# One round of eight small matmuls for the first Fourier stage of the second tokens' pairs, over other PSUM banks

## The chip, the cores and the metric

The kernel runs on one core of one Trainium2 chip. The metric is the device time of one execution in microseconds (us); lower is better. A change of 0.5% of this kernel's time is about 3.65 us.

## The reference

One token sequence (2048 tokens of 448 features) is normalised, and three things are added up: the input, a state-space convolution of the normalised input, and a gated linear unit of it. The convolution is written with a Fourier transform of double length. Cut to what matters:

```python
def _A_ref(u, log_A_real, A_imag, C_real, C_imag, log_dt, D_skip):   # S4D convolution
    dt = jnp.exp(log_dt)
    A = -jnp.exp(log_A_real) + 1j * A_imag
    C = (C_real + 1j * C_imag) * dt[:, None]
    P = jnp.exp((A * dt[:, None])[:, :, None] * pos[None, None, :])
    K = 2.0 * jnp.einsum("dn,dnl->dl", C, P).real                    # (448, 2048) from 256 modes
    Kf, Uf = jnp.fft.rfft(K, 2 * L), jnp.fft.rfft(u_t, 2 * L)
    y = jnp.fft.irfft(Uf * Kf, 2 * L)[:, :, :L]
    return y.transpose(0, 2, 1) + u * D_skip

def _B_ref(x, w_gate, w_up, w_down):                                 # gated unit, 448 -> 1792 -> 448
    return (sigmoid(x @ w_gate) * (x @ w_up)) @ w_down

x = A_u                                     # (1, 2048, 448)
xn = _layernorm(x)
return x + _A_ref(xn, ...) + _B_ref(xn, ...)
```

## The kernel before

Two generators, `conv()` for the convolution and `glu()` for the gated unit, are drawn from in turn, by fixed shares of progress, so that their instructions are recorded interleaved. The compiler's scheduler then puts each engine's instructions in one order and hands out the PSUM and SBUF buffers; on the chip each engine runs its own list in that order, and semaphores hold it where data or a buffer is missing. A matmul in float32 shows as two records in the trace.

**The gated unit.** The tokens go in two halves of 1024, each as two groups of 512 (`t` = 0, 1). `gate` (line 705) makes for one block of 128 hidden columns the two products `gu` of 512 tokens (11 matmuls each), `th` (tanh, ScalarE), `hf` (VectorE), and the split of `hf` into `hh` (ScalarE) and `hl` (VectorE). The down projection (`po`, line 817) sums over a group of blocks per 128 tokens, and VectorE adds it to `acc` (line 822). At the end of the first half lies one group, `cross`, of two blocks, in which the second 1024 tokens are also prepared, two blocks of 128 tokens ("a pair", b = 8, 10, 12, 14) at a time: `pair_norm` (normalise), `pair_turn` (transposes at line 209, split at lines 215 to 222) and `pair_first`, the subject here. `pair_first` 8 and 10 are called between the two products of a gate, 12 and 14 between two blocks of the down projection.

**The kernel of the convolution.** `kgen` makes the convolution's kernel in 56 steps, and is under way during `cross`. A step has: phases into the two-bank PSUM tile `tr` (two matmuls, line 532), from which ScalarE makes the tile `S` of sines (lines 540, 541, 542, which read `tr`, then 543); VectorE's three products `Et`, `Et`, `Ft` (lines 597 to 599); 64 records of small matmuls into `ko` (line 613). Powers `pm` (line 446) and magnitudes `me`, `mf` (GpSimd, line 510; two squarings by ScalarE, line 523) come ahead of them. There are two tiles `S` (`S0`, `S1`), so the sines of a step wait until VectorE is done with those of two steps before. Every fourth step `ko` is copied to `ks`, and `first_stage` (line 558) turns it with 32 small matmuls into the banks `kp` and `kq`.

**PSUM.** The eight banks are: four of the tag `gu`, which the gates, the down projection, `kq`, `pair_turn` and `pair_first` share; two of `tr`; one `ko`; one `kp`.

**The first Fourier stage.** `x_first_stage(to, xn, g)` multiplies 32 of the 128 partitions (group `g`) of the two token blocks of a pair with `wx`, in two matmuls of 32 rows by 64 columns by 448. For the first 1024 tokens `x_spec` does it in two goes of two groups each, through `tr`. For the second, `pair_first` takes four `gu` banks, one a group, copies each with ScalarE (line 688), two of them into one tile `x1` that shares its buffer with the gate weights (`wraw`), two into tiles that share theirs with the down weights (`rd`), and ScalarE's queue issues for each copy two stores to `x1_d` (line 690), eight a pair. The spectra stage, last in the kernel, reads `x1_d`.

Of the kernel before, what the change touches and what calls it, by code (L numbers as in the profile page):

```python
# [11 lines left out]
F32 = mybir.dt.float32  # L12
# [8 lines left out]
D = 448  # L21
# [19 lines left out]
RB = 2  # L41
# [87 lines left out]
def s4d_glu_kernel(ctx, tc, io):  # L129
    nc = tc.nc  # L130
# [20 lines left out]
    wx = const.tile([128, 64], F32, name="wx")  # L151
# [26 lines left out]
    psg = ctx.enter_context(tc.tile_pool(name="psg", bufs=1, space=PSUM))  # L178
    pg = ctx.enter_context(tc.tile_pool(name="pg", bufs=1, side="left"))
# [91 lines left out]
    def row(b, g):  # L271
        return 32 * (b // 4 % 2) + 8 * g + 4 * (b // 8) + b % 4

    def x_first_stage(to, xn, g):

        s = slice(32 * g, 32 * g + 32)
        for i in range(2):
            nc.tensor.matmul(to[64 * i : 64 * i + 64], wx[s], xn[i][s], start=True, stop=True)

    def x_spec(xn, b0):  # L280

        for p in range(2):
            x1 = slots[("x1a", "x1b", "x1c")[x1s[0] % 3]]
            x1s[0] += 1
            ps = psc[-1].tile([128, 2, 512], F32, name="tr", bufs=1)
            with tc.issue_after(glu_mm[0].ins):
                for j in range(2):
                    x_first_stage(ps[:, j, :D], xn, 2 * p + j)
            nc.scalar.copy(x1, ps[:, :, :D])
            for i in range(2):  # L290
                r = row(b0 + i, 2 * p)
                nc.sync.dma_start(x1_d[:, r : r + 9 : 8], x1[64 * i : 64 * i + 64])
            yield WX
# [386 lines left out]
    def pair_first(b, xns):  # L680

        x1 = pg.tile([128, 2, D], F32, name="x1", tag="wraw", bufs=1)
        pss = [psg.tile([128, 512], F32, name="gu", bufs=4) for _ in range(4)]
        for g in range(4):
            x_first_stage(pss[g][:, :D], xns, g)
        for g in range(4):
            to = x1[:, g] if g < 2 else pg.tile([128, D], F32, name="x1", tag="rd", bufs=RB)
            nc.scalar.copy(to, pss[g][:, :D])
            for i in range(2):
                nc.scalar.dma_start(x1_d[:, row(b + i, g)], to[64 * i : 64 * i + 64])  # L690

# [34 lines left out]
    def glu():  # L726
        stores, later = [], []
        for half in range(2):
# [4 lines left out]
            for fs_ in ORDER[half]:  # L733
# [8 lines left out]
                if cross:  # L742
                    xts = {b: pair_load(b) for b in range(8, 16, 2)}
                    step = lambda f_, b: f_(b, xts[b])
                    mid = [(pair_norm, 8), None, (pair_first, 8), (pair_first, 10)]
                    end = [(), ((pair_turn, 8), (pair_norm, 10)), ((pair_turn, 10), (pair_norm, 12)), ((pair_turn, 12), (pair_norm, 14))]
                    downs = {(0, 0): (pair_first, 12), (0, 1): (pair_turn, 14), (0, 3): (pair_first, 14)}
# [360 lines left out]
    xq, psc, raws, acl, marks, slots, pqs = list(x_first), [], [], [], [None, None], {}, []  # L1108
# [6 lines left out]
    while any(g is not None for g in gens):  # L1115
# [3 lines left out]
        i = min(live, key=lambda i: done[i] / total[i])  # L1119
# [33 lines left out]
```

## Time and profile before

| | |
|---|---|
| median of 3 runs | 729.95 us (728.79 to 732.33) |
| profiled execution | 734.12 us |
| its span, first to last instruction | 732.3 us |
| mean granted TensorE clock | 0.973 |
| TensorE busy | 680.6 us, 93% |
| VectorE busy | 567.3 us, 77% |
| ScalarE busy | 420.8 us, 57% |
| GpSimd busy | 377.3 us, 52% |

Shares of the whole span mix stages with different limits: the start loads and normalises, then the gated unit runs beside `kgen` (to about 540 us), then beside the spectra stage. The four calls of `pair_first` run between 296 and 346.4 us. PE in the lines of the profile is TensorE's matmuls, PEld its weight loads, DVE VectorE, ACT ScalarE, POOL GpSimd, SP SyncE; a "q" behind a name is the engine's own instruction queue, which also issues transfers.

### The profile page before, as it was taken

Reading aid. Unit: us, or ns where it says so; the run is one execution under the profiler, and the core shown is the slowest. Engines: PE = TensorE matmul, PEld = TensorE weight load, DVE = VectorE, ACT = ScalarE, POOL = GpSimd, SP = SyncE. Lnnn points to the kernel's source line nnn. Section 1 sums busy time; section 2 is a strip of 40 time slices with the busy share of each in tenths; the row PEclk is TensorE's granted clock in tenths of the full one; section 3 lists DMA queues with packets and bytes.
Section 4 is the critical chain, followed back from the end, with each engine's and each line's share of the span. In section 5 each row is a group of like instructions: output and inputs, shape, how many; then the busy total and the mean of one; then the engine's idle time right before and its main releaser. Section 6 shows DMA issues by size and latency. Waiting matters only on the chain.

```text
span 732.3 us, 19070 instructions
## 1 busy us (share of the span) xinstructions
PE 680.6 (93%) x7780; PEld 535.8 (73%) x7780; DVE 567.3 (77%) x776; ACT 420.8 (57%) x650; POOL 377.3 (52%) x423
## 2 busy tenths in 40 slices
PE   2898799997998999999999999999999999989994
PEld 1665688786876887566878887888877787766783
DVE  5799996799989999998498988986955555654553
ACT  3646364678587778997388678768633312313310
POOL 2120027799887788786557856767843003251001
PEclk9998899999999999997999999999999999999998
DMA  9946328435314544553952322232359999999756
GB/s 202 227 111 199 80 82 276 146 104 186 126 51 154 176 155 136 157 151 120 267 179 98 93 97 96 76 102 96 70 160 294 265 233 239 217 227 250 178 138 162
DMA packets 93287, 116.76 MB, mean 159 GB/s; under 512 B 12177, under 2 KB 81169, under 8 KB 92945
## 3 DMA queue, kind: packets, MB, share of 16 engines
q1 hardware_dynamic: 83888, 95.08, 48.1%
q10 hardware_dynamic: 6736, 14.57, 6.3%
q0 software_dynamic: 2576, 5.90, 3.3%
q8 instruction: 61, 1.00, 0.6%
q14 instruction: 26, 0.20, 0.1%
HBM read 70.75 MB, written 44.76 MB: 158 GB/s over the span
## 4 chain that ended last, share of the span: by engine, by line
PE 60%; DVE 17%; DMA 6%; ACT 6%; issue 5%; SPq 3%; POOL 1%; ACTq 0%; DVEq 0%; POOLq 0%
PE gu L705 23%; PE po L817 15%; PE sp L899 7%; PE ko L613 6%; PE pv L926 4%; PE tr L532 3%; DVE Ft L599 2%; DVE Et L598 2%; DVE Et L597 2%; DVE hl L723 2%; DMA acc_d<-acc 1%; DMA sx<-x_d 1%; DVE wl L760 1%; DVE hf L716 1%; PE kq L558 1%
## 5 line engine op out<-in xcount | busy, mean ns | idle before, releaser
L510 POOL TENSOR_TENSOR me<-me,pm 128x32 f32<-128x32 f32 (+1 forms) x168 | 144.4, 860 | 88.4 <-DVE Et L598 76.3
L510 POOL TENSOR_TENSOR mf<-mf,pm 128x64 f32<-128x64 f32 (+1 forms) x112 | 119.5, 1067 | 4.9
L705 PE MATMUL gu<-xh,wh 128*128 128x512 f32 x336 | 101.1, 407 | 3.0 <-ACT xh L218 2.8
L705 PE MATMUL gu<-xh,wl 128*128 128x512 f32 x336 | 96.1, 394 | 0.0
L705 PE MATMUL gu<-xl,wh 128*128 128x512 f32 x336 | 95.1, 390 | 0.0
L817 PE MATMUL po<-dh,hh 128*128 128x448 f32 x224 | 86.6, 387 | 3.3 <-DVE acc L822 2.5
L597 DVE TENSOR_TENSOR Et<-me,S 128x1024 f32<-128x1024 f32 x56 | 81.6, 1457 | 8.0 <-ACT S L543 4.1
L598 DVE TENSOR_TENSOR Et<-me,S 128x1024 f32<-128x1024 f32 x56 | 79.8, 1425 | 8.2 <-ACT me L523 5.8
L599 DVE TENSOR_TENSOR Ft<-mf,S 128x1024 f32<-128x1024 f32 x56 | 78.9, 1408 | 7.3 <-ACT S L543 4.4
L817 PE MATMUL po<-dl,hh 128*128 128x448 f32 x224 | 84.3, 376 | 0.0
L817 PE MATMUL po<-dh,hl 128*128 128x448 f32 x224 | 83.6, 375 | 0.0
L540 ACT ACTIVATE S<-tr 128x1024 f32<-128x1024 f32 x56 | 57.7, 1030 | 42.7 <-PE tr L532 37.4
L721 ACT CAST hh<-hf 128x512 fp32r<-128x512 f32 x56 | 35.0, 626 | 80.4 <-DVE hf L716 62.8
L705 PEld LDWEIGHTS gu<-xh,wh 128*128 128x128 f32 x336 | 61.8, 191 | 21.7 <-ACT xh L218 4.2
L705 PEld LDWEIGHTS gu<-xh,wl 128*128 128x128 f32 x336 | 63.3, 189 | 15.2 <-DVE pl L306 0.7
L613 PEld LDWEIGHTS ko<-Et,Ft 128*32 128x32 f32 x3584 | 54.1, 111 | 27.4 <-issue 16.6
L705 PEld LDWEIGHTS gu<-xl,wh 128*128 128x128 f32 x336 | 63.1, 188 | 14.1 <-issue 0.7
L613 PE MATMUL ko<-Et,Ft 128*32 128x64 f32 x3584 | 64.2, 222 | 9.0 <-DVE Et L597 4.6
L716 DVE SCALAR_TENSOR_TENSOR hf<-th,gu 128x512 f32<-128x512 f32 x56 | 38.1, 681 | 36.4 <-PE gu L705 27.3
L822 DVE SCALAR_TENSOR_TENSOR acc<-po,acc 128x448 f32<-128x448 f32 x80 | 48.5, 615 | 22.8 <-PE po L817 22.7
L543 ACT ACTIVATE S<-S,hpi 128x1024 f32<-128x1024 f32 x56 | 65.6, 1171 | 0.0
L723 DVE TENSOR_TENSOR hl<-hf,hh 128x512 fp32r<-128x512 f32 x56 | 48.9, 874 | 16.6 <-ACT hh L721 16.6
(196 smaller groups left out, 1293.9 us busy)
## 6 DMA issues: line engine op xcount, KB each, us to landing
sk_d<-sk ACTq DMA_DIRECT2D x14, 512.0 KB
sx<-x_d SPq DMA_DIRECT2D x32, 224.0 KB
skl<-sk_d SPq DMA_DIRECT2D x16, 448.0 KB
vp<-v_d SPq DMA_DIRECT2D x16, 448.0 KB
v_d<-vt SPq DMA_DIRECT2D x62, 112.0 KB
wt_d<-wh SPq DMA_DIRECT2D x9, 512.0 KB
wt_d<-wl SPq DMA_DIRECT2D x9, 512.0 KB
wl<-wt_d SPq DMA_DIRECT2D x9, 512.0 KB
```

The source lines that it names most:

```text
L510: ins = nc.gpsimd.tensor_tensor(m[:, :, w + a : 2 * w : n], m[:, :, a:w:n], par(base + i).unsqueeze(2).to_broadcast([128, 4 * DC, w // n]) ...
L540: nc.scalar.activation(rows(cs), pv, AF.Abs)
L543: sins[:] = [nc.scalar.activation(cs, cs, AF.Sin, scale=-TWO_PI, bias=hpi)]
L597: v.tensor_tensor(Et[:, :, :, 32:64], two(me[:, :, 32:64]), S[:, 1::-1], ALU.mult)
L598: v.tensor_tensor(Et[:, :, :, 0:32], two(me[:, :, 0:32]), S[:, 1:3, :, ::-1], ALU.mult)
L599: fts[:] = [v.tensor_tensor(Ft, two(mf), S[:, 3:5], ALU.mult)]
L613: nc.tensor.matmul(ko[32 * j : 32 * j + 32, sl], Ft[:, cc, DC * h + 4 * q + j], Et[:, cc, DC * h + 4 * q + j], start=(k == 0), stop=(k == ...
L705: glu_mm[:] = [nc.tensor.matmul(ps, a_, b_, start=(n == 0), stop=(n == len(mm) - 1))]
L723: v.tensor_tensor(hl, hf, hh, ALU.subtract)
L817: glu_mm[:] = [nc.tensor.matmul(po, a_[:, bs], w_, start=(n == 0), stop=(n == 3 * fc - 1))]
L822: v.scalar_tensor_tensor(acc[:, b], po, 0.5, acc[:, b], ALU.mult, ALU.add)
L899: mm = nc.tensor.matmul(to, tb[:kk, t, 64 * c : 64 * c + 64], rhs, start=True, stop=True, skip_group_check=True,)
```

## The change

The stage's eight matmuls of a pair go out one behind the other, into four banks: both of the phases' tile `tr`, `kp`, and one of the tag `gu`. Groups 0 and 1 are copied by one ScalarE instruction over both banks of `tr` (128x896), groups 2 and 3 by one each. Their eight stores stay on ScalarE's queue: four follow the copy of `tr`, two each of the others. `issue_after` puts groups 2 and 3 behind group 1 in TensorE's order.

```diff
         for i in range(2):
-            nc.tensor.matmul(to[64 * i : 64 * i + 64], wx[s], xn[i][s], start=True, stop=True)
+            mm = nc.tensor.matmul(to[64 * i : 64 * i + 64], wx[s], xn[i][s], start=True, stop=True)
+        return mm
...
     def pair_first(b, xns):
 
         x1 = pg.tile([128, 2, D], F32, name="x1", tag="wraw", bufs=1)
-        pss = [psg.tile([128, 512], F32, name="gu", bufs=4) for _ in range(4)]
+        two = psc[-1].tile([128, 2, 512], F32, name="tr", bufs=1)
+        kp = psc[-1].tile([128, 512], F32, name="kp", bufs=1)
+        pss = [two[:, 0], two[:, 1], kp, psg.tile([128, 512], F32, name="gu", bufs=4)]
+        x_first_stage(pss[0][:, :D], xns, 0)
+        mm = x_first_stage(pss[1][:, :D], xns, 1)
+        with tc.issue_after(mm.ins):
+            for g in (2, 3):
+                x_first_stage(pss[g][:, :D], xns, g)
+        nc.scalar.copy(x1, two[:, :, :D])
         for g in range(4):
-            x_first_stage(pss[g][:, :D], xns, g)
-        for g in range(4):
-            to = x1[:, g] if g < 2 else pg.tile([128, D], F32, name="x1", tag="rd", bufs=RB)
-            nc.scalar.copy(to, pss[g][:, :D])
+            if g > 1:
+                to = pg.tile([128, D], F32, name="x1", tag="rd", bufs=RB)
+                nc.scalar.copy(to, pss[g][:, :D])
+            else:
+                to = x1[:, g]
             for i in range(2):
                 nc.scalar.dma_start(x1_d[:, row(b + i, g)], to[64 * i : 64 * i + 64])
```

## The prediction

> **What bounds the kernel now.** First the page, for engine shares and the chain that ended last.
>
> ```profile
> PE 680.6 (93%) x7780; PEld 535.8 (73%) x7780; DVE 567.3 (77%) x776; ACT 420.8 (57%) x650; POOL 377.3 (52%) x423
> PE 60%; DVE 17%; DMA 6%; ACT 6%; issue 5%; SPq 3%; POOL 1%; ACTq 0%; DVEq 0%; POOLq 0%
> ```
>
> TensorE bounds the whole, but these are means over stages. So next the busy time by stretches: around the four calls of `pair_first`, and from there to the end of `kgen`. Columns: stretch, length, busy time (instructions) of PE, PEld, DVE, ACT, POOL, then the granted clock, DMA share, GB/s.
>
> ```profile
> 296.10:301.72 5.62, 4.28 (x85) 1.84 (x84) 5.56 (x8) 4.54 (x10) 5.38 (x7) 1.00 0.42 137
> 301.72:307.07 5.35, 5.35 (x84) 4.18 (x85) 5.32 (x6) 5.30 (x11) 4.38 (x5) 1.00 0.57 144
> 307.07:314.33 7.26, 7.26 (x98) 4.19 (x96) 7.18 (x9) 7.06 (x11) 5.16 (x6) 1.00 0.57 187
> 314.33:346.31 31.98, 29.85 (x419) 20.66 (x416) 28.53 (x35) 27.50 (x47) 24.76 (x28) 0.84 0.47 145
> 331.00:341.00 10.00, 9.93 (x113) 8.66 (x114) 8.44 (x11) 5.98 (x9) 8.45 (x12) 0.50 0.21 48
> 346.30:540.00 193.70, 191.94 (x2918) 158.40 (x2916) 158.10 (x166) 136.05 (x195) 130.16 (x152) 1.00 0.39 122
> ```
>
> From 296.10 to 346.31 us PE is busy 46.74 of 50.21 us and DVE 46.59: two engines near their limit, ACT not far behind (44.40). After 346.3 PE is busy 191.94 of 193.70 us, so a delay of PE at 346.3 is not won back; it reaches the end. The question is therefore when PE comes to the down projection at 346.31 that follows the last call. The built order of the changed kernel agrees with the old one before 296 us and, apart from small shifts over the next 25 us or so, behind that point; between them the same work stands in another order.
>
> **What goes: five rounds.** The first row below is the busy time of the 64 stage records in that window, the others are PE's time line (start, duration, group).
>
> ```profile
> 296.00:346.50 50.50, 9.15 (x64) 2.01 (x64) 0.90 0.49 150
> 296.42 0.97 PE L278 MATMUL gu<-xt,wx 32*64 32x448 f32 x4 [0.24 <-DVE xl L216]
> 300.60 0.99 PE L278 MATMUL gu<-xt,wx 32*64 32x448 f32 x12
> 309.67 1.34 PE L278 MATMUL gu<-xt,wx 32*64 32x448 f32 x8
> 345.41 0.97 PE L278 MATMUL gu<-xt,wx 32*64 32x448 f32 x4 [0.20 <-ACT x L688]
> ```
>
> Four records (one group) take 0.97 us and twelve (three groups) 0.99: groups in other rows of the array run together, and the time is that of a round. Now there are nine rounds, 9.15 us. Four rounds of sixteen records, at 1.0 us by the row of twelve (1.34 at worst), take 4.0 to 5.4: **5.1 us less** of PE. ACT's 16 copies become 12, about equal in sum (of two banks 0.91, of one 0.53, in rows below).
>
> **What comes: a wait in front of the first round.** A round now needs `tr` empty. In the built order round 8 stands behind steps K1, K2 and K3 of `ko` and their phases T1, T2, T3 (named in the order from 296 us), and the second gate product, G1, behind the round. T3's `S` goes into the tile that K3's products still read. So the chain is DVE's products, ACT's three sines, round, gate. Rows of PE, DVE, ACT:
>
> ```profile
> 297.64 0.43 PE L613 MATMUL ko<-Et,Ft 128*32 128x64 f32 x16 [0.25 <-DVE Ft L599]
> 299.94 0.73 PE L532 MATMUL tr<-sel,ph 128*128 128x512 f32 x2
> 301.72 0.96 PE L705 MATMUL gu<-xh,wh 128*128 128x512 f32 x3
> ...
> 303.67 0.84 PE L705 MATMUL gu<-xl,wh 128*128 128x512 f32 x3
> 304.90 0.88 PE L209 MATMUL gu<-ident,xt 128*128 128x128 f32 x6
> 324.12 1.10 PE L613 MATMUL ko<-Et,Ft 128*32 128x64 f32 x64
> 331.07 1.93 PE L613 MATMUL ko<-Et,Ft 128*32 128x64 f32 x64 [1.63 <-DVE Et L597]
> 299.89 1.33 DVE L597 TENSOR_TENSOR Et<-me,S 128x1024 f32<-128x1024 f32 x1
> 301.70 1.36 DVE L599 TENSOR_TENSOR Ft<-mf,S 128x1024 f32<-128x1024 f32 x1
> 297.19 0.68 ACT L523 ACTIVATE me<-me 128x512 f32<-128x512 f32 x1
> 300.71 1.02 ACT L540 ACTIVATE S<-tr 128x1024 f32<-128x1024 f32 x1 [1.08 <-PE tr L532]
> 301.63 1.02 ACT L541 ACTIVATE S<-tr 128x1024 f32<-128x1024 f32 x1
> 302.53 0.60 ACT L542 ACTIVATE S<-tr 128x512 f32<-128x512 f32 x1
> 303.84 1.19 ACT L543 ACTIVATE S<-S,hpi 128x1024 f32<-128x1024 f32 x1
> ```
>
> K1 and T1 stay (to 300.67). K2 waits for `Ft` at 302.5 (`Et` ends 301.2, `Ft` 1.3): PE idle 1.9. K2 1.1, T2 0.7: 304.3. T3 must wait until ACT has read T2 out (1.0 + 1.0 + 0.6): 306.9, idle 2.6. DVE meanwhile does small pieces to 304.1, then `Et`, `Et`, `Ft` of K3 (1.3 each): 308.0. ACT then needs two sines (2.0), a square (0.7) and the third sine (0.6): **round 8 at 311.5**, PE idle 2.2 more; it ends at 312.5, or 313.4 at half clock. Today G1 starts at 301.72. From 296.2 to 312.5 PE has under 8 us of work.
>
> The clock: a wait of 1.63 us at 331.07, in sparse work, was followed by ten us at a granted 0.50, in which a `ko` step took 1.93 instead of 1.10. In the new stretch the waits are longer and the work sparser, so I expect half clock from about 306 until G1 has run some 3 us: G1 with its six transposes (2.65, from 301.72 to the last three's end less their overlap, + 0.88) ends at about 318.3 instead of 316.7, 1.6 us lost. The Trainium skill, TensorE: Matmul & The Clock Gate, section Part 1: The HAM clock gate, ties the drop to an idle window of about 3.4 us; by that none of these waits would drop the clock, and the sum would be some 1.6 us lower. The row at 331.07 speaks against taking it so.
>
> **What comes: transfers issued in bunches on ACT.** The old order mostly puts stores singly or in twos between ACT's instructions. The new one puts four behind the copy of `tr`, with the copy of `kp`, of `gu`, the casts of the transposes and the next sines behind them. What six in a row cost shows at the last call:
>
> ```profile
> 44.23 0.91 ACT L289 COPY x1ab<-tr 128x896 f32<-128x896 f32 x1
> 346.29 3.71 ACTq L690 DMA_DIRECT2D x_d<-x  x6
> 350.04 0.53 ACT L688 COPY x<-gu 128x448 f32<-128x448 f32 x1 [2.97 <-DMA x_d<-x]
> 327.63 1.15 PE L558 MATMUL kp<-wk,ks 64*64 64x64 f32 x32
> 346.38 5.30 PE po L817 x24
> ```
>
> 0.6 us each, and ACT's next copy waited 2.97 us behind them though its bank was filled at 346.4. The Trainium skill, DMA: Bandwidth & Descriptors, section Issuing engines are not separate DMA queues, calls issuing time "usually small relative to the DMA itself". These rows show it as an engine's idle time, and by the skill's sentence the next paragraph's waits would be nearly nothing.
>
> The walk on, at 0.55 to 0.6 us a store. *Round 8 out:* copy of `tr` to 314.1, stores to 316.4, other copies to 317.4, casts to 318.6; DVE's `xl` splits, `hf`, `hl`, `Ft` of K5 to 322.9. PE: K4 with two transposes 320.3, T4 321.0, G2 323.6, K5 324.7, round 10 325.7, G3 with transposes 329.2, T5 329.9, K6 330.9. *Round 10 out:* ACT reaches its copies only at 327.7 (sines, power, tanh, normalise, square): 329.1; six stores to 332.1; cast 332.7; the `gu` copy 333.2, which frees the bank that the down projection takes next: PE idle 2.3. That block (1.33, a quarter of 5.30 for 24) and two transposes end at 334.9. ACT: casts to 334.5, sines of T5 to 336.9, then round 12 may start: idle 2.0. *Round 12 out:* ends 337.9; copy, four stores and the copy of `kp` to 342.4, which `first_stage` needs (2 x 1.1, two of the row of 32 records): PE idle 1.4; casts held by four more stores to 345.7, then two transposes, idle 1 more; T6 at 346.6 to 347.3; ACT's copies of `kp`, `kq`, then three sines: 350.4. PE's two down blocks and K7 fit under that. **Round 14 at 350.4 to 351.2, the down projection at 351.4 to 352.2**, against 346.31: **+5.1 to +5.9**.
>
> **The same as a sum.** Rounds -5.1. The old half clock goes: ten us at 0.50, 9.93 of them busy, hold up to 5 us of excess, I take 4.5; two drops come, 1.6 at G1 and about 1 around 336 to 345, the rest hidden under ACT's waits: -1.9. Waits: old 50.21 - 46.74 = 3.5; new 2.1 (around K1) + 1.9 + 2.6 + 2.2 + 0.6 + 2.3 + 2.0 + 1.4 + 1.0 = 16.1: +12.6. Together **+5.6 us**. Behind 346 us the chain goes through the store of `acc`:
>
> ```profile
> 352.36 10.42 DMA acc_d<-acc
> ```
>
> It begins after the down projection, so it moves with PE, and ACT's own delay is covered there, since ACT idles for that transfer in any case. GpSimd's weight loads wait for the stores of the last `x1`; they now stand ahead of a chain of `me`, and that step of `ko` has moved behind later gate matmuls by about as much: nothing counted, up to 2 us if that cover fails. The profiled execution took 734.12 us (span 732.3 and 1.8 around it), 4.2 more than the median of the three runs; 734.12 + 5.5 is 739.6 on its own scale, and the shift on the median gives 729.95 + 5.5 = **735.5 us**, which I forecast. About 0.5% (3.65 us) is what a measurement of this kernel tells from no change.
>
> **Rivals.** *(1) Faster: the stores hold nobody and the rounds are kept.* If ACT's copies slip past the stores, the 6.7 us of waits behind rounds 10 and 12 go, and DVE's row is the floor: 46.59 of 50.21 us, so at most 3.6 us faster. With G1 also at full clock my walk gives 343.7, 2.6 us faster: 727.3. It decides at ACT's copies after round 10: at 333 they hold the down projection, at 330.5 they don't. For it: DVE and ACT are near full now, so waits of PE may cost nothing. Against: the 2.97 us row, and that PE waits already before 312. This rival is what the Trainium skill's sentence on issuing, quoted above, amounts to. Its chance is 0.15: 0.06 within 0.5%, and 0.09 beyond, where also the waits that DVE has after 337 us shrink or the stretch behind 346 us gains. *(2) No change:* the stores hold ACT half as long; 345.4 to 349.9, so 729 to 733.5: 0.21. *(3) The clock stays at half through the second sparse stretch,* as it did for ten us from 331: another 3 to 5 us, 738.5 to 741: 0.14. *(4) The round isn't one:* sixteen records take 2 us instead of 1, 4 us more at most: inside the range.
>
> **How the numbers follow.** The forecast (ACT's bunches and the first wait, 733.6 to 738.5) has 0.50. With rival 3's 0.14, slower by over 0.5% has 0.64; the same, rival 2's 0.21 and rival 1's 0.06, 0.27; faster 0.09. The range goes from 728, in the upper half of rival 1, to 741, the end of rival 3.
>
> **What would show it.** Right: L278 in four groups of sixteen records at about 1 us; the first starting near 311 to 312, with ACT's sines ended just before; PE's clock near 0.5 around 306 to 316; ACT idle "<-DMA x_d<-x" for 2 us or more behind the copies of `tr`; down blocks or rounds waiting for ACT at 331 to 351; PE's stretch from 296.1 to the down projection after the last round near 55.7 us. Wrong: ACT's copies running beside the stores, round 8 before 309, or that stretch below 50 us. Then the waits were under DVE's cover.

## The result, and the profile after

The changed kernel takes 750.18 us (median of 4 runs, 750.15 to 752.32) against 731.14 us for the kernel before on the same chip (728.79 to 734.88): a ratio of 1.0263, 95% interval 1.0213 to 1.0313. It is slower, as forecast, but by 19 us where the forecast had 5.5; 750 lies outside the range. The profiled execution of the changed kernel took 750.16 us (span 748.3, mean clock 0.960), 16.0 more than that of before. The lines of the code ahead of `pair_first` stand one further down (phases `tr` L533, sines L541 to L544, `ko` L614), those behind it ten (gate L715, down projection L827); the copies are L692 (`tr`) and L696, the stores L700.

The page of the changed kernel, its parts 1 and 2 (busy shares; granted clock in fortieths of the span):

```profile
PE 680.2 (91%) x7780; PEld 537.4 (72%) x7780; DVE 566.8 (76%) x776; ACT 422.4 (56%) x646; POOL 374.7 (50%) x423
PEclk9998899999999999598989999999999999999998
```

The work of every engine is as before; what grew is idle time, and the clock falls to 0.5 in the one slice around 308 us. The same kernel by stretches (columns as in the prediction); the first is the whole from the last gate product ahead of the rounds to the down projection behind them:

```profile
295.80:358.10 62.30, 45.26 (x677) 31.38 (x676) 44.37 (x52) 41.05 (x65) 37.12 (x44) 0.78 0.37 109
295.80:312.40 16.60, 9.60 (x203) 6.55 (x202) 14.69 (x16) 13.72 (x22) 14.89 (x18) 0.62 0.15 49
300.00:301.00 1.00, 0.79 (x2) 0.07 (x1) 1.00 (x2) 0.17 (x1) 1.00 (x1) 0.50 0.00 0
304.00:316.00 12.00, 8.84 (x114) 5.46 (x106) 10.27 (x9) 9.68 (x14) 10.53 (x12) 0.50 0.06 14
334.16:355.00 20.84, 14.24 (x113) 10.24 (x114) 8.54 (x14) 10.80 (x18) 6.63 (x11) 0.76 0.43 126
376.00:386.00 10.00, 6.11 (x42) 4.47 (x34) 5.14 (x8) 8.37 (x13) 0.84 (x1) 0.66 0.99 227
```

62.30 us where before had 50.21: 12.1 more, with 1.5 less of work on PE. DVE is busy for 44.37 of these 62.30, so it is no floor any more. Between 334.16 and 355.00 no engine is busy for more than 14.24 of 20.84 us. The last row shows a second loss, behind the part that the prediction walked: the two spans differ by 16.0 us, so some 4 arise there.

PE's time line of the changed kernel, the rounds and the rows behind a wait (297.34 is the first `ko` step, K1, and 299.63 its phases, T1):

```profile
297.34 0.53 PE L614 MATMUL ko<-Et,Ft 128*32 128x64 f32 x20 [1.47 <-DVE Ft L600]
299.63 1.16 PE L533 MATMUL tr<-sel,ph 128*128 128x512 f32 x2
302.55 1.94 PE L614 MATMUL ko<-Et,Ft 128*32 128x64 f32 x64 [1.76 <-DVE Ft L600]
308.16 1.22 PE L533 MATMUL tr<-sel,ph 128*128 128x512 f32 x2 [2.52 <-ACT S L543]
312.42 1.02 PE L278 MATMUL tr<-xt,wx 32*64 32x448 f32 x4 [0.64 <-ACT S L543]
314.15 0.80 PE L715 MATMUL gu<-xh,wh 128*128 128x512 f32 x1
...
326.06 0.60 PE L278 MATMUL tr<-xt,wx 32*64 32x448 f32 x4
327.00 0.50 PE L715 MATMUL gu<-xh,wh 128*128 128x512 f32 x1
...
334.16 0.74 PE L827 MATMUL po<-dh,hh 128*128 128x448 f32 x1 [1.78 <-ACT x L696]
340.06 0.60 PE L278 MATMUL tr<-xt,wx 32*64 32x448 f32 x4 [2.86 <-ACT S L543]
341.79 0.57 PE L827 MATMUL po<-dl,hh 128*128 128x448 f32 x1
350.57 0.41 PE L209 MATMUL gu<-ident,xt 128*64 128x128 f32 x2 [2.99 <-DVE xl L219]
357.16 0.60 PE L278 MATMUL tr<-xt,wx 32*64 32x448 f32 x4
358.10 0.47 PE L827 MATMUL po<-dh,hh 128*128 128x448 f32 x1
...
380.16 1.22 PE L533 MATMUL tr<-sel,ph 128*128 128x512 f32 x2 [3.90 <-ACT S L543]
```

A round is one stretch of work: 0.94 us at full clock (326.06 to 327.00), 1.73 at half (312.42 to 314.15). The long waits between 330 and 351 us (1.78, 2.86 and 2.99 us) lead back to ACT's time line, the last by way of DVE, whose `xl` reads what ACT has cast:

```profile
315.19 2.45 ACTq L700 DMA_DIRECT2D x_d<-x  x4
317.68 0.53 ACT L696 COPY x<-kp 128x448 f32<-128x448 f32 x1 [2.52 <-DMA x_d<-x]
...
329.33 3.71 ACTq L700 DMA_DIRECT2D x_d<-x  x6
333.08 0.58 ACT L215 CAST xh<-gu 128x512 fp32r<-128x512 f32 x1 [3.35 <-issue]
...
334.63 0.62 ACT L731 CAST hh<-hf 128x512 fp32r<-128x512 f32 x1 [0.25 <-DVE xl L216]
337.08 0.45 ACTq L700 DMA_DIRECT2D x_d<-x  x1
337.58 1.02 ACT L541 ACTIVATE S<-tr 128x1024 f32<-128x1024 f32 x1 [2.33 <-PE gu L209]
...
344.77 0.53 ACT L696 COPY x<-kp 128x448 f32<-128x448 f32 x1 [2.55 <-DMA x_d<-x]
345.33 3.50 ACTq L700 DMA_DIRECT2D x_d<-x  x4
348.88 0.58 ACT L215 CAST xh<-gu 128x512 fp32r<-128x512 f32 x1 [3.14 <-DMA x_d<-x]
```

Two things are to be seen. In bunches of four or six, ACT stands idle for 2.5 to 3.4 us until the last is issued. In the kernel before, most stores went out while ACT was still computing, these two beside the sine that ran from 303.84 to 305.03 and the instruction behind it:

```profile
304.08 1.25 ACTq L690 DMA_DIRECT2D x_d<-x  x2
```

And the last store of the second round, at 337.08, is issued 1.8 us after ACT's cast ended (335.25), with the sines of the next step behind it: the 2.33 is put down to `gu L209`, but in the instruction order the store comes ahead of the sine. That store waits for a completion counter (a semaphore that tells that a transfer has landed): the trace has ACT's transfers on eight of them by turns, and this one names the counter of the store issued at 330.46, which landed at 337.06. Two 512 KB weight loads that SP issued at 329.81 and 330.50 were under way at the same time; that they made that store late is argued, not shown. The single issues, grouped by line, first of the changed kernel and then of before (min/median/max in ns):

```profile
L700 ACTq DMA_DIRECT2D x_d<-x x32: 452/607/1718, 315.2 to 364.2; - x32
```

```profile
L690 ACTq DMA_DIRECT2D x_d<-x x32: 452/528/1012, 299.4 to 351.7; - x32
```

Behind 358 us, ACT's time line in the changed kernel:

```profile
370.94 1.03 ACT L541 ACTIVATE S<-tr 128x1024 f32<-128x1024 f32 x1 [0.81 <-PE tr L533]
...
376.27 0.32 ACTq L241 DMA_DIRECT2D acc<-in_A_u_dram  x1
376.63 0.62 ACT L731 CAST hh<-hf 128x512 fp32r<-128x512 f32 x1 [4.66 <-DMA acc_d<-acc]
376.64 1.36 ACTq L241 DMA_DIRECT2D acc<-in_A_u_dram  x3
378.60 1.02 ACT L542 ACTIVATE S<-tr 128x1024 f32<-128x1024 f32 x1
```

The second sine of a step follows the first by 7.7 us, because a load of the next `acc` (L241) now stands between them on ACT's queue, and waits for the store of the old one (`acc_d<-acc`). PE then waits 3.9 us, at 380.16, until the step's third sine has read `tr` and the next phases can go in, and the mean clock from 376 to 386 is 0.66. In the kernel before, the sines of that step stood ahead of these loads.

### The profile page after: what moved, and what is told of

It is laid out like the page before. It is cut to its first block, busy times and chain, and to the rows that moved or that the text cites. A ratio compares the mean times of both kernels' runs of the same rounds, so it can differ in the third digit from the quotient of the medians.

```text
span 748.3 us, 19062 instructions
## 1 busy us (share of the span) xinstructions
PE 680.2 (91%) x7780; PEld 537.4 (72%) x7780; DVE 566.8 (76%) x776; ACT 422.4 (56%) x646; POOL 374.7 (50%) x423
## 4 chain that ended last, share of the span: by engine, by line
PE 45%; DMA 4%; ACT 4%; DVE 3%; issue 1%; ACTq 1%; POOL 0%; POOLq 0%; DVEq 0%; SPq 0%
PE gu L715 16%; PE po L827 10%; PE sp L909 6%; PE ko L614 4%; PE pv L936 4%; PE tr L533 3%; DMA sx<-x_d 2%; DMA acc<-in_A_u_dram 1%; DMA x_d<-x 1%; ACTq L700 1%; PE kp L559 1%; ACT S L542 1%; PE kq L559 1%; PE tr L278 1%; ACT S L543 0%
## 5 line engine op out<-in xcount | busy, mean ns | idle before, releaser
L715 PE MATMUL gu<-xh,wh 128*128 128x512 f32 x336 | 102.5, 410 | 3.3 <-ACT xh L218 3.3
L715 PE MATMUL gu<-xh,wl 128*128 128x512 f32 x336 | 96.9, 396 | 0.0
L715 PE MATMUL gu<-xl,wh 128*128 128x512 f32 x336 | 95.7, 391 | 0.0
L827 PE MATMUL po<-dh,hh 128*128 128x448 f32 x224 | 86.9, 388 | 5.1 <-DVE acc L832 2.5
L827 PE MATMUL po<-dl,hh 128*128 128x448 f32 x224 | 85.0, 379 | 0.0
L600 DVE TENSOR_TENSOR Ft<-mf,S 128x1024 f32<-128x1024 f32 x56 | 80.8, 1444 | 5.0 <-ACT S L544 2.9
L827 PE MATMUL po<-dh,hl 128*128 128x448 f32 x224 | 84.1, 377 | 0.0
L541 ACT ACTIVATE S<-tr 128x1024 f32<-128x1024 f32 x56 | 57.5, 1027 | 39.4 <-PE tr L533 36.5
L715 PEld LDWEIGHTS gu<-xh,wh 128*128 128x128 f32 x336 | 62.3, 193 | 22.4 <-issue 5.1
L715 PEld LDWEIGHTS gu<-xh,wl 128*128 128x128 f32 x336 | 63.7, 190 | 15.4 <-DVE pl L307 0.7
L614 PEld LDWEIGHTS ko<-Et,Ft 128*32 128x32 f32 x3584 | 54.5, 112 | 28.1 <-issue 15.2
L715 PEld LDWEIGHTS gu<-xl,wh 128*128 128x128 f32 x336 | 63.5, 189 | 14.3 <-issue 0.7
L614 PE MATMUL ko<-Et,Ft 128*32 128x64 f32 x3584 | 63.9, 224 | 10.3 <-DVE Ft L600 7.0
L544 ACT ACTIVATE S<-S,hpi 128x1024 f32<-128x1024 f32 x56 | 65.4, 1168 | 0.0
```

Source lines behind the costliest of these rows:

```text
L541: nc.scalar.activation(rows(cs), pv, AF.Abs)
L544: sins[:] = [nc.scalar.activation(cs, cs, AF.Sin, scale=-TWO_PI, bias=hpi)]
L600: fts[:] = [v.tensor_tensor(Ft, two(mf), S[:, 3:5], ALU.mult)]
L614: nc.tensor.matmul(ko[32 * j : 32 * j + 32, sl], Ft[:, cc, DC * h + 4 * q + j], Et[:, cc, DC * h + 4 * q + j], start=(k == 0), stop=(k == ...
L715: glu_mm[:] = [nc.tensor.matmul(ps, a_, b_, start=(n == 0), stop=(n == len(mm) - 1))]
L827: glu_mm[:] = [nc.tensor.matmul(po, a_[:, bs], w_, start=(n == 0), stop=(n == 3 * fc - 1))]
```

## The experiments

**Theory A:** the stores, issued in bunches on ACT, cost most of the loss. **Theory C:** the loads of `acc` ahead of the sines cost the rest. The rivals lay the loss on the round itself or on the bank it waits for. One execution of either kernel can lie several us from its median (the kernel before ran from 727 to 739 in these comparisons), so what counts below is the ratio to the kernel before on the same chip, with its 95% interval; it is worked out from the single runs and can differ by some tenths of a per cent from the quotient of two medians. Gains in us that follow a ratio are differences of ratios times 731. Places in a trace are read from its own first `ko` step of the stretch.

**Stores on SP instead of ACT.**

```diff
-                nc.scalar.dma_start(x1_d[:, row(b + i, g)], to[64 * i : 64 * i + 64])
+                nc.sync.dma_start(x1_d[:, row(b + i, g)], to[64 * i : 64 * i + 64])
```

> The changed kernel with its eight stores a pair issued by SP instead of ACT; nothing else differs. Theory A (the bunches of stores hold ACT, and PE waits for what ACT does late): ACT's idle times of 2.5 to 3.4 us behind the copies go, the down projection after round 10 and rounds 12 and 14 come some 8 to 10 us earlier, time about 740 to 742 us. Theory B (the wait for the phases' banks and the order that follows from it are the loss, the stores only lie beside it): 747 to 751 us. Round 8 still starts near 312 us by both.

Measured: 736.22 us, ratio 1.0071 (1.0029 to 1.0113): 14 us of the 19 are gone with this one line, more than the 8 to 10 that theory A had. PE's rounds and the stretch in its trace:

```profile
315.24 1.02 PE L278 MATMUL tr<-xt,wx 32*64 32x448 f32 x4 [0.80 <-ACT S L543]
328.08 0.61 PE L278 MATMUL tr<-xt,wx 32*64 32x448 f32 x4
335.59 0.61 PE L278 MATMUL tr<-xt,wx 32*64 32x448 f32 x4
347.19 0.61 PE L278 MATMUL tr<-xt,wx 32*64 32x448 f32 x4
```

```profile
298.70:348.13 49.43, 40.46 (x677) 28.34 (x676) 41.92 (x49) 38.56 (x62) 39.27 (x44) 0.86 0.45 120
```

49.43 us where the changed kernel took 62.30, and the kernel before 50.21 in its profiled execution and 47.65 in the control with the loads further down: nearly all of the excess up to the down projection belonged to the stores' place on ACT. The wait in front of the first round is still there. What is left lies behind, with the loads of `acc`. One that waits for a store of `acc` stands ahead of ACT's last copy, for which PE waits 3.06 us, and one ahead of a sine:

```profile
355.23 0.53 ACT L696 COPY x<-gu 128x448 f32<-128x448 f32 x1 [4.31 <-DMA x_d<-x]
355.81 0.47 PE L827 MATMUL po<-dh,hh 128*128 128x448 f32 x1 [3.06 <-ACT x L696]
368.44 1.74 ACTq L241 DMA_DIRECT2D acc<-in_A_u_dram  x4
370.22 1.15 ACT L544 ACTIVATE S<-S,hpi 128x1024 f32<-128x1024 f32 x1 [4.71 <-issue]
```

**The control: the same edit in the kernel before** (its line 690, `nc.scalar` to `nc.sync`).

> The kernel before with the stores of pair_first issued by SP instead of ACT. Theory A says that stores cost where they come in bunches; here they come singly but for the last six, so 0 to 3 us less, 728 to 731 us. Theory B says the same as no change. It is the control for the changed kernel with its stores on SP.

Measured: 732.25 us, ratio 0.9992 (0.9958 to 1.0027). SP is no better place in itself; there the stores hide on ACT.

**Loads of `acc` on GpSimd instead of ACT, stores left on ACT.**

```diff
-                    x_load(accs[q], 4 * q, 4, [nc.scalar])
+                    x_load(accs[q], 4 * q, 4, [nc.gpsimd])
```

> The changed kernel with the eight loads of the second tokens' inputs into acc issued by GpSimd instead of ACT; its stores stay on ACT. Theory C (part of the loss comes behind the last round, where a sine stands on ACT behind a load that waits for the store of acc to land, and PE waits 3.9 us for it at 376 us and then runs at half clock): 4 to 6 us less, 744 to 746 us. Theories A and B: no change but what the loads do on GpSimd's queue, 749 to 751 us.

Measured: 743.62 us, ratio 1.018 (1.0112 to 1.0249): some 6 us less than the changed kernel. The size is uncertain: one of the four executions took 750.20, and the interval meets that of the changed kernel. The rounds stay late, as theory A says (the last at 356.73, 59.7 us behind the first `ko` step; 59.8 in the changed kernel), and no wait of PE like that at 380.16 remains:

```profile
339.34 1.02 PE L278 MATMUL tr<-xt,wx 32*64 32x448 f32 x4 [4.26 <-ACT S L543]
356.73 0.61 PE L278 MATMUL tr<-xt,wx 32*64 32x448 f32 x4
```

**Both edits together.**

> The changed kernel with two edits at once: the stores of the spectra issued on SP instead of ACT, and the loads of acc issued on GpSimd instead of ACT. Theory A+C (the change loses its time in two places, in the bunches of stores on ACT up to the down projection, and behind it in loads of acc that stand on ACT ahead of a step's last sines): the two gains add, 750.2 - 13.9 - 6.6 = 729.7 us, 727 to 732, no wait of 2 us or more for a load or a store in front of a sine, and the down projection again some 56 us behind 302. Rival (one wait behind both, so that whichever edit is made frees the same time): 736 to 737, as with the stores alone.

Measured: 734.25 us, ratio 1.0014 (0.9983 to 1.0044). The gains add up nearly (14.0 and 6.1 alone, 18.2 together, by the ratios), and the excess is gone within the interval; by the median the time is 2 us above the 727 to 732 expected. The down projection comes at 347.76, 47.4 us behind the first `ko` step (with the stores alone 47.9); the "56 us behind 302" of the expectation is the place that it has in the changed kernel. No sine waits 2 us or more for a load or a store, and PE has no wait of 0.9 us or more between the first round and 400 us. The rival's 736 to 737 lies at the upper end of the interval (736.2) and above; that each edit alone frees another time and other waits speaks more clearly against it.

**The control: the loads on GpSimd in the kernel before.**

> The kernel before with the loads of acc issued on GpSimd instead of ACT. Theory C (the loads stand ahead of sines only where the change has moved them there): the kernel before gains nothing, 731 to 734 against 732.9. Rival (the loads cost ACT as much in the kernel before): 5 to 7 us faster, 726 to 728, and then the 6.6 us are not of the change.

Measured: 732.84 us, ratio 0.9996 (0.9967 to 1.0025). The loads cost nothing that can be measured until the change let them slip in front of the sines.

The two stretches without disturbed ACT, of the changed kernel with both edits and of this control, each from the last gate product to the down projection behind the rounds:

```profile
298.66:347.76 49.10, 40.81 (x677) 28.45 (x675) 40.65 (x49) 38.82 (x63) 39.81 (x44) 0.86 0.45 123
```

```profile
293.00:340.65 47.65, 45.55 (x679) 29.00 (x679) 46.58 (x53) 44.28 (x75) 40.77 (x43) 0.93 0.51 157
```

PE is busy for 4.7 us less with four rounds, so the saving is real even at the lower clock; but it idles for 8.3 us (49.10 - 40.81) instead of 2.1, and 6.8 of the 8.3 lie up to the first round. The saving goes into the waits in front of that round, which needs `tr` empty and has the second gate product behind it.

**Is it the issue or the wait for a counter? Two banks' stores merged.** Four stores of 64x448 become two of 64x2x448; six issues a round on ACT instead of eight.

```diff
+        for i in range(2):
+            r = row(b + i, 0)
+            nc.scalar.dma_start(x1_d[:, r : r + 9 : 8], x1[64 * i : 64 * i + 64])
...
-            for i in range(2):
+            for i in range(2 if g > 1 else 0):
```

> The changed kernel with the four stores of the two banks' tile written as two, each with both phases in it (64x2x448); the same bytes, six stores on ACT in a round instead of eight, the rounds where they were. In the changed kernel the last stores of the second and the fourth round also wait for the completion of an earlier transfer of the same round: there are eight completion counters, handed out in turn, and a store waits until the last transfer on its counter has landed; with six stores most of these waits are gone. Theory A1 (what costs is the 0.45 to 0.6 us of each issue): two of eight issues gone, 2/8 of the 14 us, so 746 to 747. Theory A2 (what costs most is the wait for a counter, 2 to 3 us a time): 738 to 743, and no store on ACT behind an idle time of 2 us at 334 to 337.

**Half the stores on SP,** those of the two banks; the other four stay on ACT.

```diff
-                nc.scalar.dma_start(x1_d[:, row(b + i, g)], to[64 * i : 64 * i + 64])
+                (nc.scalar if g > 1 else nc.sync).dma_start(x1_d[:, row(b + i, g)], to[64 * i : 64 * i + 64])
```

> The changed kernel with the four stores of the two banks' tile issued on SP and the four of the other two banks left on ACT: the same number of transfers and of counters, half the issues on ACT. Theory A1 (issue time): half of the 14 us, 742 to 744. Theory A2 (the counters): the last stores of a round are still on ACT and still wait, so less than half is gained, 744 to 749. Rival (only the first stores of a round hold anything, those in front of the kernels' bank's copy): all of it gained, 736 to 738.

Measured: merged 744.39 us, ratio 1.0187 (1.015 to 1.0223); half on SP 743.0 us, ratio 1.0164 (1.0123 to 1.0204). Of the merged kernel, ACT's rows of the second round and PE's third and fourth round:

```profile
332.06 0.53 ACT L699 COPY x<-gu 128x448 f32<-128x448 f32 x1 [2.41 <-issue]
332.62 0.45 ACTq L703 DMA_DIRECT2D x_d<-x  x1
333.13 0.59 ACTq L703 DMA_DIRECT2D x_d<-x  x1
```

```profile
336.52 0.81 PE L278 MATMUL tr<-xt,wx 32*64 32x448 f32 x4 [1.30 <-ACT S L543]
348.92 0.60 PE L278 MATMUL tr<-xt,wx 32*64 32x448 f32 x4
```

The last store is out at 333.7 instead of 337.5. From one event to the next, in us (starts of K1, the first `ko` step, of the four rounds, and of the down projection, from PE's time lines):

| | stores on ACT a round | K1 to 8 | 8 to 10 | 10 to 12 | 12 to 14 | 14 to down | all |
|---|---|---|---|---|---|---|---|
| changed kernel | 8 | 15.08 | 13.64 | 14.00 | 17.10 | 0.94 | 60.76 |
| merged | 6 | 14.99 | 13.36 | 10.82 | 12.40 | 0.94 | 52.51 |
| half on SP | 4 | 15.04 | 12.40 | 9.28 | 15.41 | 0.94 | 53.07 |
| all on SP | 0 | 14.99 | 12.84 | 7.51 | 11.60 | 0.94 | 47.88 |

By the whole time, merging gains 5.6 us, between the ranges of A1 and A2, and half the stores on SP 7.2 us, within A1's; each with some 4.5 us of uncertainty. In the stretch of the table, one execution each, two issues of eight less bring 8.2 of the 12.9 us that all eight cost, and four less 7.7; issue time alone (theory A1) would give 3.2 and 6.4. Waits for counters don't fill that gap. In the changed kernel the trace has one store held for a counter up to the last round, the 1.8 us at 337.08. It lies between rounds 10 and 12, where the merged kernel gains 3.2 us. Between 12 and 14 it gains 4.7 us, and there no store of the changed kernel was held for a counter: the last issue of the bunch took 1.72 us (0.94 in the merged kernel; no run shows why), and PE had more of its small blocks at half clock. So that a held store costs time is shown; that such waits cost most (theory A2) is not, and how the size splits between issue time, held stores and half clock stays open.

Behind the rounds the merged kernel still has theory C's wait: ACT's L544 stands idle for 6.08 us. The view puts this down to a load of phases, but right in front of L544 stand four loads of `acc` (368.90 to 370.65), the first of which waited for a store of `acc` that landed at 368.80.

**Stores behind all copies, in the kernel before:** `tos` collects the four tiles, and the eight stores are written behind the fourth copy.

> The kernel before with its stores written behind all four copies of a pair, rounds and banks unchanged; on ACT they then stand in twos and threes with copies between them, not in sixes and eights. Theory A (what costs is how many issues stand on ACT in one go, 0.45 to 0.6 us each): twos and threes hide as in the kernel before, 731 to 736 us. Rival (any store that is moved behind later copies holds up the first stage of the state kernels): 740 or more.

Measured: 734.0 us, ratio 1.0022 (0.9997 to 1.0047). With rounds apart, the scheduler spreads the stores into twos and threes, and they hide. It is a weak test, as no bunch of four or more formed before the last pair.

**One round in four `gu` banks,** as close to before as a single round gets: four small matmuls, whose result is overwritten, hold the banks until the round is whole.

```diff
+            mm = nc.tensor.matmul(pss[g][:64, :32], wx[32 * g : 32 * g + 32], xns[0][32 * g : 32 * g + 32, :32], start=True, stop=True)
...
+            with tc.issue_after(mm.ins):
+                mm = x_first_stage(pss[g][:, :D], xns, g)
```

> One round of eight matmuls as in the change, but in the four gu banks of the kernel before, with its four copies and single stores; four small matmuls (64x32, overwritten by the round) take the banks beforehand, so that the eight stand together. If the round by itself is worth its 5 us and the banks tr and kp are the loss (theory B): 725 to 731 us. If any single round loses, since it must wait until four banks are free and holds the gate meanwhile: 735 to 745 us.

Measured: 758.44 us, ratio 1.0363 (1.0308 to 1.0419), slower still, and above both ranges. With all four `gu` banks gone gates and transposes wait; the last round starts at 361.1. Whether four full `gu` banks or the bunches are to blame it doesn't tell, as its copies and stores come close together too. It gives no sign that `tr` was the costly choice.

**Towards a faster kernel.** Stores on SP and merged, loads on GpSimd:

> The changed kernel with the stores on SP, those of the two banks merged into two, and the loads of acc on GpSimd. Theory A+C says that with the stores off ACT their number hardly counts: as with the two edits without the merging, 731 to 736. Rival (SP's own loads of phases and weights stand behind the stores and cost some us): fewer stores give it back, 726 to 730, faster than the kernel before.

Measured: 733.58 us, ratio 1.0031 (1.0001 to 1.0061): as theory A+C says, with ACT free merging brings nothing that can be measured. And both edits with a high priority for the round (unmerged):

> The changed kernel with the stores on SP, the loads of acc on GpSimd, and a high priority around the round and the copy of its two banks, which puts the later three rounds earlier on PE: the round at 326 stands half a step of transposes (T) earlier, that in front of the down projection 6 down blocks earlier. Theory A+C: with no work on ACT that the rounds push aside, 0 to 3 us less than without the priority, 727 to 732. Rival (the round then waits for the kernels' bank, which the step K still holds): 3 to 6 us more, 733 to 738.

Measured: 736.95 us, ratio 1.0028 (0.9995 to 1.0061), no gain either; the median lies in the rival's range, the ratio isn't told from that without the priority. No version here beats the kernel before.

## Why the prediction was right in sign and wrong in size

- **Rounds, -5.1 us: right.** Four rounds took 1.73, 0.94, 1.19 and 0.94 us by PE's time line, 4.8 in sum, within 4.0 to 5.4; against the 9.15 of before that is 4.4 less.
- **The wait in front of the first round: right.** Waits of 1.76 and 2.52 us at K2 and T3 (forecast 1.9 and 2.6), round 8 at 312.42 (forecast 311.5), the down block behind round 10 at 334.16 (333.2). Its reading survives the experiments: with the stores on SP, K1 to round 8 is still 14.99 us. Of the 2.2 us forecast as idle in front of round 8 only 0.64 were; the rest went into work at half clock.
- **The clock at G1: right, but it fell earlier than forecast.** It was 0.50 from 304 to 316 us, as forecast. But it was 0.50 from 300 us on already, and T1 took 1.16 us at 299.63 where such a pair takes 0.73 at full clock: the drop came 6 us earlier than forecast, ahead of the waits of 1.76 and 2.52 us. The longest wait of PE just ahead of it was 1.47 us, at 297.34; of the three us from 296 to 299 PE was busy for 1.03, so sparse work, which the forecast also named, fits better than a single long wait. No run here tells the two apart. By the idle window of about 3.4 us that the Trainium skill, TensorE: Matmul & The Clock Gate, section Part 1: The HAM clock gate, ties the drop to, no wait of PE here would have dropped the clock; in this trace it dropped all the same.
- **Stores in bunches: right mechanism, term mis-sized.** This is the step that failed. The sum had waits of 2.3, 2.0, 1.4 and 1.0 behind rounds 10 and 12, 6.7 us, at a flat 0.55 to 0.6 us a store, and about 1 us of half clock. The waits measured 1.78, 2.86, 0.74 and 2.99, 8.4 us. Forecast were 12.2 us from round 10 to 12 and 13.5 from 12 to 14; measured 14.00 and 17.10, and the down projection came at 358.10 instead of 351.4 to 352.2. From 10 to 12 the excess of 1.8 comes from the store that was held for the landing of an earlier one, which the walk had not counted. From 12 to 14 it is 3.6: a single issue took 1.72 us, and the walk's "PE's two down blocks and K7 fit under that" failed. PE's blocks ran at half clock (0.57 us a record against 0.36; mean clock 0.76 from 334 to 355), ACT's sines had read `tr` out by 355.40, and round 14 started at 357.16 behind PE's own work. Rival 3 held that last cost, but it came on top, not alone.
- **Behind 346 us, "nothing counted": wrong.** Some 4 us in the two profiles, and about 6 when the loads are moved. I followed the store of `acc` as a thing that moves with PE, and did not check what else the new order put behind the load that waits for it: two more sines that read `tr`, and the one behind them. GpSimd's weight loads, which I had given up to 2 us, are not shown as a cause: with the loads of `acc` put on their queue as well, the time fell.
- **The base: one execution.** Of the 13.5 us between the loss forecast and the one measured, 6.6 arise up to the down projection and 3.9 behind it; the other 3 are the profiled execution of before, which lay 3 us above the median. The sum took 4.5 us off for the half clock that this one execution had from 331 to 341 us. In the control with the loads on GpSimd the kernel before takes 47.65 us for its stretch instead of 50.21, so part of that 4.5 belonged to the one execution and not to the kernel.
- **Issuing as a small cost.** The Trainium skill, DMA: Bandwidth & Descriptors, section Issuing engines are not separate DMA queues, calls issuing time "usually small relative to the DMA itself". That comparison holds here: the store issued at 330.46 in 0.6 us landed 6.6 us later. But it doesn't tell what the issue costs. In this kernel moving 32 issues of 0.6 us to another engine was worth 14 us; in the kernel before, where they found gaps or ran beside other work, the same move was worth nothing that can be measured.

## What to carry to other kernels

When a change makes results come out together, look at what follows them on the copying engine's queue: stores that hid one at a time can hold that engine when they come in a bunch, and here one word, another queue, took most of the loss back. Count for each store not only its issue but what it may wait for, such as an earlier transfer that shares its completion counter. And walk the new order past the end of the edited region: any transfer that waits and has slipped ahead of compute on its engine is a new wait.

## What the runs showed of the hardware

A store's issue on ScalarE took from 0.45 to 1.72 us (median 0.61 in the changed kernel, 0.53 in the kernel before). In bunches of four or six ScalarE stood idle for 2.5 to 3.4 us; apart, a store was issued beside an instruction already under way. One store was held 1.8 us for the landing of an earlier one on its counter. TensorE's granted clock fell to 0.50 at about 300 us, when the longest wait just ahead was 1.47 us, and a round of sixteen small records took 1.73 us then, 0.94 at full clock.
